# Two attention heads' start-up reordered: the next pair's cluster steps, one addition, one batch and the padding products

## The chip, the cores and the metric

One Trainium2 chip, one core in use. The metric is the device time of one execution in microseconds (us). The kernel before takes 450.0 us (median of three runs: 449.5, 450.0 and 450.33).

## The reference, cut to what matters

Sixteen heads (2 batches of 8) of attention over 768 positions with 64 dimensions, each masked so that a query sees only keys of its own cluster. Clusters come from an argmax against 16 normed centroids. The output is sent through a top-1 mixture of 8 experts.

```python
q_assign = np.argmax(np.einsum('bhsd,hcd->bhsc', q_n, c_n), axis=-1)
k_assign = np.argmax(np.einsum('bhsd,hcd->bhsc', k_n, c_n), axis=-1)
mask = q_assign[:, :, :, None] == k_assign[:, :, None, :]
scores = scale * np.matmul(q, k.transpose(0, 1, 3, 2))
scores = np.where(mask, scores, -1000000000.0)
scores = scores - np.max(scores, axis=-1, keepdims=True)
attn = np.exp(scores)
attn = attn / (np.sum(attn, axis=-1, keepdims=True) + 1e-09)
return np.matmul(attn, v)          # then logits = x @ w_gate, one expert per row: relu(x w1) w2
```

## The kernel before, in words

The heads go in pairs (head 0 and 1 are pair 0). Operands are stored transposed, in tiles that hold a high part, correction pieces, 16 mask rows for the cluster (so that the product itself adds a large negative number where clusters differ) and one row with the negated row maximum. The tiles are called `W`, `Y1`, `Qs` and `Y0`; a number behind the name tells the head's copy apart.

For each head there are 12 tiles of *maxima*: `max_tile` (line 344) makes a 128 x 384 product `m` on TensorE (L351), and VectorE reduces it to one column of `mx` (L358). `m` lives in two pools of PSUM, `psM` with two buffers and `psS` with three; a product into a buffer waits for the reduction of the tile that held it. When a head's maxima are complete, VectorE joins them (`max_half` L370 in two halves for head 0, `max_chain` L364 for the others, `mxx`), TensorE turns them into a row (`half_row` L381, `max_rows` L391), and ScalarE writes the row into `Qs` (L382), or a DMA does (L393, L394). Only then can `st_group` (line 406) finish a score tile: product L415 from `Y1` and `W`, product L416 from `Y0` and `Qs`, and the exponential L420 on ScalarE. In `high` (L1258) ScalarE copies a head's high part. `split` makes the correction pieces: a subtraction on GpSimd (L311) and DMAs on SyncE's queue (L321).

After the exponentials come the products with the values (`pv_batch`, L441, two batches of three key tiles; one key tile takes four passes in two concurrent pairs) and the row sums: `p_add` (L426) adds two of the three key tiles of a batch on VectorE, and `sum_strips` (L467) sums over partitions on TensorE.

The clusters of a pair: `cl_scores` (L183; one step per tile of 128 positions, two products of 96 columns), then `cl_assign`, a generator of four stages on VectorE: maximum L246; comparison L249 and multiplication L251; maximum L254; comparison L259 that writes the one-hot tile `ohb`. `cl_back` turns `ohb` (L286), ScalarE scales it into `qkm` (L294), and four DMAs bring its rows into the `W` and `Y1` tiles of both heads (L300).

Nothing may be reordered by a scheduler here: `keep` pins an engine's program order, so the order of the code is the order on each engine. `prologue` (line 1171) holds the start, `opening` (line 1260) all of head 0's score groups, with the maxima of heads 0 and 1 and the first three of head 2 between them. From head 1 on, a regular loop makes one score group, one or two maxima (`ahead`) and what `hooks` lists. `first_max` (line 1253) makes a maximum of head 0, `ahead` the next one of the following heads.

`keep_warm` (line 1132) makes 128 x 128 products in fp32 that nobody reads; each shows as two passes. `WARM1`, `WARM2` and `WARM3` are their counts at `first_max`, `half_row` and the first score group.

Of the kernel before, what the change touches and what calls it, by code (L numbers as in the profile page):

```python
# [7 lines left out]
F32 = mybir.dt.float32  # L8
# [4 lines left out]
ALU = mybir.AluOpType  # L13
# [3 lines left out]
P = 128  # L17
# [6 lines left out]
def kernel(  # L24
# [13 lines left out]
    nc = tc.nc  # L38
    B, NP, _, S = qT.shape
# [3 lines left out]
    NT = S // P  # L43
# [8 lines left out]
    OOB = 1 << 16  # L52
    NA = 4
    WARM1 = 1
    WARM2 = 2
    WARM3 = 3
    G_B0, G_B1, G_TURN, G_OUT = 8, 2, 5, 11
    TWICE = {(1, 1), (1, 2), (3, 2), (3, 3)}
# [71 lines left out]
    def keep(ins):  # L130
        if held[0] and ins.ins.engine in HELD:
            tc.keep_in_program_order(ins)
# [44 lines left out]
    def cl_scores(pi, w=1, t0=0, t1=NT):  # L177
        hp = pi % NP
        if t0 == 0:
            cl[pi] = psT.tile([P, 512], F32, tag="t", name="ctp")  # L180
        for t in range(t0, t1):
            for n, nm in enumerate("qk"):
                keep(nc.tensor.matmul(  # L183
                    out=cl[pi][:, t * 64 + n * 32:t * 64 + (n + w) * 32],
                    lhsT=pair[pi][nm][:, t * P:(t + 1) * P],
                    rhs=cbs[:, hp:hp + w, :],
                    start=True,
                    stop=True,
                ))
# [98 lines left out]
    def cl_back(pi):  # L288
        cl_back_turn(pi)
        cl_back_send(pi)  # L290
# [76 lines left out]
    def max_half(h, j):  # L367
        mx = mxt[h, j] = work.tile([P, TH], F32, tag="mxp", name="mxp")
        ts = slice(j * TH, (j + 1) * TH)
        keep(nc.vector.tensor_tensor(out=mx, in0=mxt[h][:, 0, ts], in1=mxt[h][:, 1, ts], op=ALU.max))  # L370
        if j == 1:
            mxt.pop(h)

    def half_row(h, j, warm=0):
        mx = mxt.pop((h, j))
        br = MROW[h % 2]
        tp = psO.tile([P, 512], F32, tag="o", name="mtd")
        if warm:
            keep_warm(warm, tp)
        for t in range(TH):  # L380
            keep(nc.tensor.transpose(tp[0:1, t * P:(t + 1) * P], mx[:, t:t + 1], ident))  # L381
        keep(nc.scalar.activation(  # L382
            out=pick(Qs_t, h)[br:br + 1, j * HALF:(j + 1) * HALF], in_=tp[0:1, 0:HALF], func=AF.Copy, scale=-1.0
        ))
# [12 lines left out]
    pt = {}  # L397
# [23 lines left out]
            out=pt[h, u][:, slot[0], slot[1]], in_=s[:, 0:HALF], func=AF.Exp, scale=1.0 / float(D) ** 0.5  # L421
        ))

    def p_add(h, u):
        a = acc[h, u] = work.tile([P, 2, HALF], F32, tag="acc", name="acc", bufs=3)
        keep(nc.vector.tensor_tensor(out=a, in0=pt[h, u][:, 0], in1=pt[h, u][:, 1], op=ALU.add))  # L426

    def p_add_rest(h, u):
        a, b = (x.rearrange("p j n -> p (j n)") for x in (acc[h, u], pt[h, u][:, 2]))
# [702 lines left out]
    def keep_warm(n, d):  # L1132

        for _ in range(n):
            keep(nc.tensor.matmul(out=d[:, 0:P], lhsT=onef, rhs=onef, start=True, stop=True))
# [35 lines left out]
    def prologue():  # L1171
# [5 lines left out]
        load_pair(0, ("k",))  # L1177
        load_pair(1)
        nc.scalar.activation(out=nbig2, in_=onef[:, 0:1], func=AF.Sqrt)
        keep_warm(5, psM.tile([P, 512], F32, tag="m", name="warm"))  # L1180
        for lst in (W_t, Y1_t, Qs_t, Y0_t):
            zero_rows(lst, 0)
        one_row(0, 0)
# [38 lines left out]
        cl_back0("q", tq)  # L1222
        mask0("q", tq, 0, slice(0, S), nc.scalar)
        high(2)
        cl_scores(1, 3, 2, 5)
        cl_back0("k", tk)
        cl_scores(1, 3, 5, NT)
        keep_warm(2, psM.tile([P, 512], F32, tag="m", name="warm"))
        for j in range(2):
            mask0("k", tk, 0, slice(j * HALF, (j + 1) * HALF), nc.scalar)  # L1230
# [9 lines left out]
        split(2, 2)  # L1240
        for k in range(NT):
            first_max(k)
        max_half(0, 0)
        a1 = gens["c"] = cl_assign(1, nc.vector)
        for j in range(2):
# [1 line left out]
        split(2, 4)  # L1247
        for k in range(NT, NT + 2):
            first_max(k, psM, "m")
        next(a1)  # L1250
        half_row(0, 0, WARM2)

    def first_max(k, *pool):
        max_tile(0, k // 2, k % 2, *(pool or ((psS, "s") if k % 5 < 3 else (psM, "m"))), warm=WARM1 if k in (3, 4, 5) else 0)

    def high(h):
        a = MAIN[h % 2]
# [2 lines left out]
    def opening():  # L1260
        a1 = gens.pop("c")
        load_pair(2)
        for g in range(2 * NT):
            if g == 6:
                half_row(0, 1)
            if g == 9:
                cl_back(1)
            if g == 10:
                pv_batch(0, 0)
            st_group(0, g)  # L1270
            if g < 4:
                first_max(8 + g, psM, "m")
            else:
                ahead()
            if g == 0:
                next(a1)
            if g == 3:
                max_half(0, 1)
            if g in (4, 6):
                next(a1, None)  # L1280
            if g == 8:
                high(3)
        split(3, 0, high=False)
        ahead(2)
        ahead(2, None, psS, "s")
        p_add(0, 0)
        p_add(0, 1)
        pv_batch(0, 1, range(1))
        max_rows(1)
        split(3, 1)  # L1290
        pv_batch(0, 1, range(1, TH))
        split(3, 2)
        split(3, 3)
        ahead(2)
        ahead(1, None, psS, "s")
        sum_strips(0)
        sum_evict(0)
        pv_evict(0)

# [4 lines left out]
    def ahead(n=1, at=None, *pool):  # L1304
        for _ in range(n):
            if maxima:
                m, k = maxima.pop(0)
                max_tile(m, k // 2, k % 2, *pool)
                if k == 2 * NT - 1:
                    max_chain(m)  # L1310
                    if at is not None:
                        rows_at[at + 2] = m
# [104 lines left out]
```

## Time and profile before

| What | Value |
|---|---|
| median of three runs | 450.0 us |
| the profiled execution | 449.91 us |
| its span | 448.1 us |
| TensorE busy | 431.6 us, 96% of the span |
| VectorE busy | 323.1 us, 72% |
| ScalarE busy | 273.8 us, 61% |
| GpSimd busy | 157.0 us, 35% |
| mean granted TensorE clock | 0.994 |

The span runs from the first to the last instruction; 1.8 us of the execution's time lie around it. PE is TensorE, DVE VectorE, ACT ScalarE, POOL GpSimd and SP SyncE. Matmuls are pipelined: a row shows a product from its start to its modelled end, so rows overlap, and what one product costs is read from start to start.

### The profile page before, as it was taken

How to read it: one execution, taken by the hardware profiler on the slowest of the kernel's cores; microseconds unless marked ns; L12 is line 12 of the kernel's file. 1: busy time of each engine (PE TensorE's matmuls, PEld its weight loads, DVE VectorE, ACT ScalarE, POOL GpSimd, SP SyncE). 2: the span in 40 equal slices, each digit the busy share in tenths (PEclk: the TensorE clock that was granted, in tenths of full speed). 3: DMA queues.
4: the chain of work that ended last, by engine and by line, in shares of the span. 5: the costliest groups of instructions: out<-in, count | busy, mean ns of one | idle time of the engine just before them, and what ended most of it. 6: DMA issues, size and time to landing. Idle time of an engine off the chain costs nothing. (4 is left out here: it accounts for less than half of the span.)

```text
span 448.1 us, 8089 instructions
## 1 busy us (share of the span) xinstructions
PE 431.6 (96%) x2776; PEld 343.2 (77%) x2776; DVE 323.1 (72%) x680; ACT 273.8 (61%) x550; POOL 157.0 (35%) x213
## 2 busy tenths in 40 slices
PE   8899999999999999999999998999999999999993
PEld 8755676676766767667665776999999999999972
DVE  4777968878788788888856644778777778786421
ACT  5655665756656557576665334668686868686330
POOL 7844665675655753573220500001010101011010
PEclk9999999999999999999999999899999999999999
DMA  6454476382763945347222367468787887975010
GB/s 194 126 150 151 105 236 215 86 292 81 213 217 104 308 145 156 81 126 225 68 98 88 144 221 233 139 219 259 250 262 251 247 260 229 281 242 187 27 40 19
DMA packets 31224, 78.14 MB, mean 174 GB/s; under 512 B 4678, under 2 KB 5024, under 8 KB 31172
## 3 DMA queue, kind: packets, MB, share of 16 engines
q1 hardware_dynamic: 26196, 61.18, 46.3%
q0 software_dynamic: 4832, 16.15, 9.7%
q8 instruction: 29, 0.48, 0.4%
q14 instruction: 23, 0.19, 0.2%
q10 hardware_dynamic: 144, 0.16, 0.1%
HBM read 50.46 MB, written 16.76 MB: 150 GB/s over the span
## 5 line engine op out<-in xcount | busy, mean ns | idle before, releaser
L358 DVE TENSOR_REDUCE mx<-m 128x1 f32<-128x384 f32 x192 | 102.5, 552 | 36.1 <-PE m L351 35.6
L420 ACT ACTIVATE pf<-s 128x384 f32<-128x384 f32 x192 | 89.5, 494 | 44.6 <-PE s L416 38.1
L142 DVE TENSOR_TENSOR ws<-wraw,ws 128x1024 fp32r<-128x1024 f32 x64 | 78.3, 1223 | 26.6 <-ACT ws L136 26.1
L697 POOL DMA_INDIRECT out_dram<-y,row x17 | 17.9, 1052 | 170.1 <-DMA row<-xd 79.7
L415 PE MATMUL s<-W,Y 112*128 112x384 f32 (+1 forms) x192 | 73.2, 381 | 0.0
L986 PE MATMUL g<-xc,ws 128*128 128x416 f32 x224 | 71.5, 379 | 1.5 <-DVE yT L995 0.6
L986 PE MATMUL g<-hc,ws 128*128 128x416 f32 x224 | 69.5, 371 | 0.0
L351 PE MATMUL m<-Y,W 112*128 112x384 f32 (+1 forms) x192 | 66.4, 353 | 2.0 <-DVE mx L358 1.4
L136 ACT ACTIVATE ws<-wraw 128x1024 fp32r<-128x1024 f32 x64 | 67.1, 1049 | 0.3 <-issue 0.2
L416 PE MATMUL s<-Qs,Y 97*128 97x384 f32 (+1 forms) x192 | 64.9, 338 | 0.4 <-ACT Qs L382 0.4
L441 PE MATMUL o<-pf,v 128*64 128x384 f32 x360 | 64.9, 495 | 0.0
L987 PE MATMUL g<-xc,ws 128*128 128x208 f32 x224 | 58.8, 262 | 1.8 <-issue 1.8
L987 PE MATMUL g<-hc,ws 128*128 128x208 f32 x224 | 57.9, 259 | 0.0
L415 PEld LDWEIGHTS s<-W,Y 112*128 112x128 f32 (+1 forms) x192 | 36.3, 189 | 16.7 <-issue 14.3
L994 ACT ACTIVATE pt<-g 128x208 f32<-128x208 f32 x84 | 27.4, 339 | 34.9 <-PE g L987 34.7
L432 POOL TENSOR_TENSOR acc<-acc,pf 128x256 f32<-128x256 f32 x39 | 29.6, 785 | 53.9 <-DVE acc L426 38.5
L986 PEld LDWEIGHTS g<-xc,ws 128*128 128x128 f32 x224 | 42.9, 192 | 3.6 <-issue 2.4
L987 PEld LDWEIGHTS g<-xc,ws 128*128 128x128 f32 x224 | 43.6, 195 | 2.0 <-issue 2.0
L441 PEld LDWEIGHTS o<-pf,v 128*64 128x64 f32 x360 | 23.4, 136 | 28.1 <-issue 23.5
L987 PEld LDWEIGHTS g<-hc,ws 128*128 128x128 f32 x224 | 42.8, 191 | 0.0
L986 PEld LDWEIGHTS g<-hc,ws 128*128 128x128 f32 x224 | 42.1, 188 | 0.4
L351 PEld LDWEIGHTS m<-Y,W 112*128 112x128 f32 (+1 forms) x192 | 35.9, 188 | 8.4 <-DVE mx L358 4.8
(210 smaller groups left out, 698.2 us busy)
## 6 DMA issues: line engine op xcount, KB each, us to landing
wraw<-in_w_dram SPq DMA_DIRECT2D x64, 512.0 KB, 4.3
xd<-z POOLq DMA_DIRECT2D x7, 780.0 KB, 6.0
row<-xd SPq DMA_DIRECT2D x18, 260.0 KB, 3.2
qv<-in_qT_dram SPq DMA_DIRECT2D x8, 384.0 KB
kv<-in_kT_dram SPq DMA_DIRECT2D x8, 384.0 KB, 3.6
Y<-Y SPq DMA_DIRECT2D x32, 96.0 KB, 2.2
Qs<-W SPq DMA_DIRECT2D x16, 192.0 KB, 6.8
v<-in_v_dram SPq DMA_DIRECT2D x8, 384.0 KB, 5.0
```

Of the source, the lines that this page charges most:

```text
L136: keep(nc.scalar.activation(out=w[:, 0], in_=raw[c], func=AF.Copy))
L142: keep(nc.vector.tensor_tensor(out=w[:, 1], in0=t, in1=w[:, 0].bitcast(F32), op=ALU.subtract))
L351: keep(nc.tensor.matmul(out=m[:, 0:HALF], lhsT=W[0:KA[h % 2], t * P:(t + 1) * P], rhs=Y1[0:KA[h % 2], j * HALF:(j + 1) * HALF], start=True ...
L358: keep(nc.vector.tensor_reduce(out=mxt[h][:, j, t:t + 1], in_=m[:, 0:HALF], axis=AX.X, op=ALU.max))
L415: keep(nc.tensor.matmul(out=s[:, 0:HALF], lhsT=Y1[0:ka, ks], rhs=W[0:ka, qs], start=True, stop=False))
L416: keep(nc.tensor.matmul(out=s[:, 0:HALF], lhsT=Y0[0:kb, ks], rhs=Qs[0:kb, qs], start=False, stop=True))
L420: keep(nc.scalar.activation(out=pt[h, u][:, slot[0], slot[1]], in_=s[:, 0:HALF], func=AF.Exp, scale=1.0 / float(D) ** 0.5))
L432: keep((nc.vector if u else nc.gpsimd).tensor_tensor(out=a[:, c:c + w], in0=a[:, c:c + w], in1=b[:, c:c + w], op=ALU.add))
L441: keep(nc.tensor.matmul(out=ot[h][j * D:(j + 1) * D, 0:HALF], lhsT=vt[h // 2][:, h % 2, kt, :], rhs=pf[:, n, j], start=(kt == 0), stop=(kt ...
L986: nc.tensor.matmul(out=o, lhsT=w[0], rhs=x.rearrange("p o n -> p (o n)"), start=start, stop=False)
L987: nc.tensor.matmul(out=o[:, 0:RW], lhsT=w[1], rhs=x[:, 0], start=False, stop=stop)
L994: nc.scalar.activation(out=t, in_=o[:, RW:2 * RW], func=AF.Copy)
```

## The change

In `prologue` two of the six steps of `cl_scores` for pair 1 move: the step with index 4, which stood ahead of the turned keys (`cl_back0("k", tk)`), and the one with index 5 behind them. They now stand behind the third and the fifth maximum of head 0. The first stage of `cl_assign` for pair 1 moves from behind the eighth maximum to behind the twelfth; the stages behind it move too. The ninth maximum of head 0 moves ahead of the first `half_row` and into the pool `psS`. In `opening` `ahead` is left out at two of the groups, and one tile is put into the first batch of value products. That batch now stands before `cl_back(1)`; the second batch is cut two to one around `max_rows(1)`, where it was one to two. `sum_strips(0)` stands ahead of the three maxima of head 2. `p_add(0, 0)` goes to GpSimd in three pieces of 256 columns. `high(3)` and the first subtraction of `split(3, 0)` follow group 8.

Of the padding, one fp32 product is added at the start, `WARM1` is used at one maximum instead of three, and in `half_row` twelve products of 32 columns in bf16 take the place of two fp32 ones; the second `half_row` gets twelve too.

```diff
-    WARM2 = 2
+    WARM2 = 12
...
-        if warm:
-            keep_warm(warm, tp)
+        for _ in range(warm):
+            keep(nc.tensor.matmul(out=tp[:, 0:32], lhsT=oneb, rhs=oneb[:, 0:32], start=True, stop=True))
...
-    def p_add(h, u):
+    def p_add(h, u, eng=nc.vector):
         a = acc[h, u] = work.tile([P, 2, HALF], F32, tag="acc", name="acc", bufs=3)
-        keep(nc.vector.tensor_tensor(out=a, in0=pt[h, u][:, 0], in1=pt[h, u][:, 1], op=ALU.add))
+        o, x, y = (t.rearrange("p j n -> p (j n)") for t in (a, pt[h, u][:, 0], pt[h, u][:, 1]))
+        w = S if eng is nc.vector else 256
+        for c in range(0, S, w):
+            keep(eng.tensor_tensor(out=o[:, c:c + w], in0=x[:, c:c + w], in1=y[:, c:c + w], op=ALU.add))
...
-        keep_warm(5, psM.tile([P, 512], F32, tag="m", name="warm"))
+        keep_warm(6, psM.tile([P, 512], F32, tag="m", name="warm"))
...
-        cl_scores(1, 3, 2, 5)
+        cl_scores(1, 3, 2, 4)
         cl_back0("k", tk)
-        cl_scores(1, 3, 5, NT)
...
         for k in range(NT):
             first_max(k)
+            if k in (2, 4):
+                cl_scores(1, 3, 3 + k // 2, 4 + k // 2)
...
-        next(a1)
+        first_max(NT + 2, psS, "s")
         half_row(0, 0, WARM2)
...
-warm=WARM1 if k in (3, 4, 5) else 0)
+warm=WARM1 if k == 4 else 0)
...
         for g in range(2 * NT):
             if g == 6:
-                half_row(0, 1)
-            if g == 9:
-                cl_back(1)
-            if g == 10:
-                pv_batch(0, 0)
-            st_group(0, g)
-            if g < 4:
-                first_max(8 + g, psM, "m")
-            else:
-                ahead()
-            if g == 0:
-                next(a1)
-            if g == 3:
-                max_half(0, 1)
-            if g in (4, 6):
-                next(a1, None)
-            if g == 8:
-                high(3)
-        split(3, 0, high=False)
+                half_row(0, 1, WARM2)
+            if g == 10:
+                pv_batch(0, 0, range(2))
+                ahead()
+                pv_batch(0, 0, range(2, TH))
+                cl_back(1)
+            st_group(0, g)
+            if g < 3:
+                first_max(9 + g, psM, "m")
+            elif g not in (5, 8):
+                ahead()
+            if g == 2:
+                max_half(0, 1)
+                next(a1)
+            if g in (4, 7):
+                next(a1)
+            if g == 8:
+                next(a1, None)
+                high(3)
+                split(3, 0, high=False)
+            if g == 9:
+                p_add(0, 0, nc.gpsimd)
         ahead(2)
         ahead(2, None, psS, "s")
-        p_add(0, 0)
         p_add(0, 1)
-        pv_batch(0, 1, range(1))
+        pv_batch(0, 1, range(2))
         max_rows(1)
         split(3, 1)
-        pv_batch(0, 1, range(1, TH))
+        pv_batch(0, 1, range(2, TH))
         split(3, 2)
         split(3, 3)
+        sum_strips(0)
         ahead(2)
         ahead(1, None, psS, "s")
-        sum_strips(0)
```

VectorE, from the join of head 0's first six maxima (`mxp`) to the one-hot tile of pair 1 (`ohb`), before:

```order
L370 TENSOR_TENSOR mxp<-mx 128x3
L358 TENSOR_REDUCE mx<-m 128x1 x2
L246 TENSOR_REDUCE cmx<-ctp 128x24
L358 TENSOR_REDUCE mx<-m 128x1
L249 TENSOR_TENSOR ceq<-ctp,cmx 128x384
L251 TENSOR_TENSOR ceq<-ceq,c16b 128x384
L358 TENSOR_REDUCE mx<-m 128x1 x3
L370 TENSOR_TENSOR mxp<-mx 128x3
```

And now:

```order
L370 TENSOR_TENSOR mxp<-mx 128x3
L358 TENSOR_REDUCE mx<-m 128x1 x6
L370 TENSOR_TENSOR mxp<-mx 128x3
L246 TENSOR_REDUCE cmx<-ctp 128x24
L358 TENSOR_REDUCE mx<-m 128x1 x2
L249 TENSOR_TENSOR ceq<-ctp,cmx 128x384
L251 TENSOR_TENSOR ceq<-ceq,c16b 128x384
```

The three cluster operations that stood between the reductions of head 0 stand behind all of them.

TensorE, from the last five maxima of head 1 to the first score group of head 1, before (`o` is the value product, `mtp` the turned maxima of head 1, `rsp` the row sums):

```order
L351 MATMUL m<-Y_103,W_99 128x384 x5
L441 MATMUL o<-pf,v 64x384 x2
L391 MATMUL mtp<-cs,mxx 6x128
L441 MATMUL o<-pf,v 64x384 x4
L351 MATMUL m<-Y_102,W_98 128x384 x3
L467 MATMUL rsp<-acc,onef 32x384 x2
L467 MATMUL rsp<-pf,onef 32x384 x2
L467 MATMUL rsp<-acc,onef 32x384 x2
L467 MATMUL rsp<-pf,onef 32x384 x2
L415 MATMUL s<-W_99,Y_103 128x384
```

And now:

```order
L351 MATMUL m<-Y_103,W_99 128x384 x5
L444 MATMUL o<-pf,v 64x384 x4
L391 MATMUL mtp<-cs,mxx 6x128
L444 MATMUL o<-pf,v 64x384 x2
L470 MATMUL rsp<-acc,onef 32x384 x2
L470 MATMUL rsp<-pf,onef 32x384 x2
L470 MATMUL rsp<-acc,onef 32x384 x2
L470 MATMUL rsp<-pf,onef 32x384 x2
L351 MATMUL m<-Y_102,W_98 128x384 x3
L415 MATMUL s<-W_99,Y_103 128x384
```

Two value products moved ahead of the turned maxima, and the row sums moved ahead of head 2's first maxima.

SyncE's queue, from the first load for head 3 to the row of maxima of head 1, before:

```order
L321 DMA Qs_108<-W_100 64x768
L300 DMA W_98<-qkm 16x768
L300 DMA Y_102<-qkm 16x768
L300 DMA W_100<-qkm 16x768
L300 DMA Y_104<-qkm 16x768
L321 DMA W_100<-ql 32x768
L394 DMA Qs_107<-mr 1x6x128
```

And now:

```order
L321 DMA Qs_108<-W_100 64x768
L321 DMA W_100<-ql 32x768
L321 DMA Qs_108<-ql 32x768
L300 DMA W_98<-qkm 16x768
L300 DMA Y_102<-qkm 16x768
L300 DMA W_100<-qkm 16x768
L300 DMA Y_104<-qkm 16x768
L394 DMA Qs_107<-mr 1x6x128
```

Two DMAs that wait for GpSimd's subtraction `ql` of head 3 now stand ahead of the four that bring the cluster rows.

## Rows read from the trace of the kernel before

**Rows 1.** Busy time by stretch, all engines, 50 to 100 us (busy and instructions)

```profile
50.00:100.00 50.00, 49.87 (x331) 33.77 (x330) 40.47 (x84) 30.65 (x64) 34.41 (x48) 1.00 0.59 183
```

**Rows 2.** Timeline of TensorE, 8 to 52 us: start, duration, instruction, [idle before <- what ended it]

```profile
14.21 0.64 PE L1135 MATMUL warm<-onef 128*128 128x128 f32 x4
14.60 0.90 PE L351 MATMUL m<-Y,W 112*128 112x384 f32 x3
...
18.26 0.49 PE L381 MATMUL mtd<-cs,mxp 128*1 128x128 f32 x3
...
21.06 0.34 PE L416 MATMUL s<-Qs,Y 97*128 97x384 f32 x1
22.39 0.44 PE L351 MATMUL m<-Y,W 112*128 112x384 f32 x1 [0.99 <-DVE mx L358]
22.67 0.34 PE L415 MATMUL s<-W,Y 112*128 112x384 f32 x1
22.84 0.34 PE L416 MATMUL s<-Qs,Y 97*128 97x384 f32 x1
...
26.42 0.39 PE L351 MATMUL m<-Y,W 128*128 128x384 f32 x1
26.84 0.51 PE L286 MATMUL ctb<-idb,ohb 128*128 128x128 bf16 x6
...
32.66 0.87 PE L441 MATMUL o<-pf,v 128*64 128x384 f32 x4
34.16 0.27 PE L391 MATMUL mtp<-cs,mxx 128*6 128x128 f32 x1 [0.64 <-DVE mxx L364]
...
37.96 0.44 PE L415 MATMUL s<-W,Y 128*128 128x384 f32 x1
```

**Rows 3.** Timeline of VectorE, same stretch

```profile
15.06 2.88 DVE L358 TENSOR_REDUCE mx<-m 128x1 f32<-128x384 f32 x6 [2.23 <-PE m L351]
17.98 0.16 DVE L370 TENSOR_TENSOR mxp<-mx 128x3 f32<-128x3 f32 x1
...
21.05 0.82 DVE L251 TENSOR_TENSOR ceq<-ceq,c16b 128x384 bf16<-128x384 bf16 x1
...
23.46 0.53 DVE L370 TENSOR_TENSOR mxp<-mx 128x3 f32<-128x3 f32 x1
...
34.02 1.82 DVE L426 TENSOR_TENSOR acc<-pf 128x768 f32<-128x768 f32 x2
```

**Rows 4.** Timeline of ScalarE, same stretch

```profile
13.79 1.03 ACT L279 ACTIVATE Y<-ctk,nbig 16x384 fp32r<-16x384 bf16 x2 [0.30 <-PE ctk L269]
```

**Rows 5.** Timeline of TensorE around 174 us: five small products in bf16

```profile
173.97 0.28 PE L640 MATMUL gps<-goh,oneb 128*128 128x80 bf16 x5
174.11 0.20 PE L641 MATMUL gps<-run,oneb 128*128 128x96 bf16 x1
```

**Rows 6.** Timeline of GpSimd, 8 to 52 us

```profile
23.20 2.10 POOL L311 TENSOR_TENSOR Y<-kv,Y 64x256 fp32r<-64x256 f32 x3
...
49.27 2.42 POOL L432 TENSOR_TENSOR acc<-acc,pf 128x256 f32<-128x256 f32 x3 [1.34 <-DVE cm L254]
```

**Rows 7.** Timeline of SyncE's queue, same stretch: issue of a DMA

```profile
29.02 0.52 SPq L300 DMA_DIRECT2D W<-qkm  x1
```

**Rows 8.** DMA issues, 5 to 60 us: issuer, count, KB each, median us to landing

```profile
W<-qkm SPq DMA_DIRECT2D x4, 48.0 KB, 2.0
```

**Rows 9.** Timeline of TensorE: three rows of the start, one around 278 us

```profile
1.05 2.50 PE L1135 MATMUL warm<-onef 128*128 128x128 f32 x10 [1.05 <-DVE nbig L1174]
3.83 0.58 PE L1144 MATMUL nps<-onef,csq 128*128 128x1 f32 x2 [0.28 <-DVE csq L1141]
...
8.57 1.90 PE L222 MATMUL ctp<-cbs,kv 128*128 128x128 f32 x12
...
278.20 0.37 PE L987 MATMUL g<-xc,ws 128*128 128x208 f32 x1 [1.78 <-issue]
```

**Rows 10.** Busy time by stretch, 279 to 283 us; the eighth figure is the granted clock

```profile
279.00:283.00 4.00, 4.00 (x19) 3.89 (x17) 2.17 (x4) 1.91 (x5) 0.00 (x0) 0.57 0.19 38
```

More of the change, by code (lines that the diff above doesn't have):

```diff
@@ L1249, in prologue @@
             first_max(k, psM, "m")
-        next(a1)
+        first_max(NT + 2, psS, "s")
         half_row(0, 0, WARM2)
     def first_max(k, *pool):
-        max_tile(0, k // 2, k % 2, *(pool or ((psS, "s") if k % 5 < 3 else (psM, "m"))), warm=WARM1 if k in (3, 4, 5) else 0)
+        max_tile(0, k // 2, k % 2, *(pool or ((psS, "s") if k % 5 < 3 else (psM, "m"))), warm=WARM1 if k == 4 else 0)
     def high(h):
```

## Prediction

> **What bounds the kernel now.** I read the busy time by stretch first. From 50 to 100 us TensorE is busy for 49.87 of 50 us [rows 1], while VectorE has 40.47 and ScalarE 30.65. So the regular part is TensorE's, and what a changed opening saves arrives at the end as an earlier start of that part. I take its start to be the first score product of head 1, at 37.96 [rows 2]; everything that the change moves lies ahead of it. Next I read TensorE's timeline up to there [rows 2], from start to start. Two products that follow each other without a wait stand 0.17 us apart (22.67, 22.84); right behind a wait the distance is 0.28 (22.39, 22.67). The reader should look for the places where more than that passes: 21.06 to 22.39, where a maximum waits for VectorE; 26.42 to 26.84, where the turn of the one-hot tile waits; and 32.66 to 34.16, where the turn of head 1's maxima waits. VectorE's timeline [rows 3] tells why. A reduction comes every 0.465 us ((2.88 - 0.55) / 5 for the six from 15.06, with 0.55 for the last), but between those of head 0 stand cluster operations, the longest of 0.82 at 21.05.
>
> **The change, part by part.** The sum is made against the profiled execution, 449.91 us, 0.09 below the median of 450.0. I lay the new order along the old durations.
>
> *A. Up to the turn of head 0's first six maxima*, which starts at 18.26 [rows 2]. One cluster step fewer stands ahead of the turned keys. ScalarE's key mask began at 13.79, behind an idle of 0.30 that the turned keys ended [rows 4]. It can start near 13.50, and the first maximum, which needs its first half (1.03 / 2), near 13.50 + 0.52 + 0.05 = 14.1. It started at 14.60, right behind four padding passes [rows 2], so VectorE is 0.5 early at first. But two cluster steps (four passes of 0.10 each; the four from 14.21 to 14.60 give the pass) now stand between the maxima, against two fp32 pads of two passes that go. The sixth product starts near 16.7, its reduction ends near 17.7, the join of 0.16 near 17.87. TensorE is then through with the ninth maximum and the twelve small products too (near 17.9), so the turn starts near 17.93. **Gain 0.33**, bounds 0 and 0.5.
>
> *B. From there to the second half row of head 0.* The last maxima of head 0 no longer find cluster operations between their reductions. The 1.33 from 21.06 to 22.39 becomes 0.17, and the distance behind it 0.17 instead of 0.28: 1.27. The ninth maximum is already made: 0.17. The second join ended at 23.46 + 0.53 = 23.99 [rows 3], where TensorE, with five more products of 0.175 behind 22.84, was ready at 23.72; that wait, 0.33 with 0.06 for the hand-over, goes. (The twelfth product now starts near 22.39 - 0.33 - 1.16 - 0.17 - 0.35, one score group fewer being ahead of it, so at 20.4; 0.44, a reduction of 0.55 and a join of at most 0.53 lead to 21.9, and TensorE arrives near 22.3.) The second twelve small products cost their time: 0.028 each, from five between 173.97 and 174.11 [rows 5], so 0.34. **Gain 1.27 + 0.17 + 0.33 - 0.34 = 1.43.** The trace has no such product in this place. One bound is 0; the other an fp32 pass of 0.10, with which all twenty-four cost 1.7 more. I take 0.028, since those five rows are bf16 against the same tile of ones.
>
> *C. The one-hot tile.* From 26.42 to 26.84 TensorE lost 0.42 - 0.18 = 0.24 [rows 2]. Now a score group (0.35) and the first value batch (2.3 with its inserted maximum) stand ahead of the turn, which comes near 26.84 - 1.76 - 0.24 + 0.35 + 2.3 = 27.5. VectorE's nine operations of about 0.5 behind the second join end near 26.5, so the wait goes. **Gain 0.24.** The price is that the cluster rows leave later. ScalarE's scaling of the turned tile, about 1.03 as for the same 768 columns at 13.79, ends near 29.1. On SyncE's queue two DMAs stand ahead that need GpSimd's subtraction for head 3. It starts behind `high(3)`, which stands ahead of the turn, so it ends at the latest 2.10 [rows 6] behind 27.5, at 29.6. Two issues and two for the first cluster rows, 0.52 or a little more each [rows 7], lead to 32.0 at the latest, and the row lands 2.0 behind its issue's start [rows 8], by 33.5. Head 2's first maximum needs them near 34.7. I charge nothing; 1.2 us are left.
>
> *D. Turned maxima of head 1, and the sums.* From 32.66 to 34.16 stands one key tile of value products, 0.70 with its hand-over; 0.80 was lost, 0.64 of it as the row's idle [rows 2]. A second key tile now fills 0.70. I leave 0.20 as a rest of the wait, since the join comes near 32.1. **Gain 0.60**, bounds 0 and 0.8. The first of the two additions on VectorE (1.82 for both at 34.02) [rows 3] goes to GpSimd: its three pieces take 2.42 [rows 6] and end by 32.0 at the latest. The row sums need them near 33.3, so the cover is 1.3 us.
>
> Here a rule speaks against the change. The join of three columns took 0.16 at 17.98 and 0.53 at 23.46 [rows 3], the latter while GpSimd's first piece ran from 23.20 to about 23.9 [rows 6]. So a two-input operation on VectorE can wait for a piece on GpSimd, for 0.8 at most (2.42 / 3). Until the join near 32.1 VectorE has reductions only, which read PSUM. I charge nothing, with 0.8 as the bound. The Trainium skill (SBUF — State Buffer, section "SBUF: two separate sides") calls the port that the two engines share an exclusive lock, held for a whole instruction while the other engine is blocked. The trace agrees (0.53 against 0.16); by that rule the sum stays the same unless a piece is still running at the join, and is then up to 0.8 smaller.
>
> *E. What comes back.* The first three maxima of head 2 stood ahead of the row sums, during which VectorE reduced them. Now they stand right ahead of head 1, whose next two groups make three more. The second maximum of group 1 waits for the reduction of group 0's, the fourth in line: 0.44 for the first product, 0.56 and three times 0.465 give 2.4 us, while TensorE gets there after nine products, about 1.9. Part of that wait was there before, since two maxima in a row always wait for each other. I charge 0.35 for it, and 0.10 because VectorE's remaining addition ends just when the sums want it. **Loss 0.45**, bounds 0 and 1.4 (three whole reductions).
>
> *At no cost:* the sixth padding product at the start. The ten passes from 1.05 end 0.28 ahead of the next product at 3.83, which waits for VectorE [rows 9]; two more, of some 0.21, fill the gap. If they are too long, at most 0.2 is lost.
>
> Sum: 0.33 + 1.43 + 0.24 + 0.60 - 0.45 = 2.15. So **449.91 - 2.15 = 447.8 us**. The uncertain terms together (A, the small products, D, E) leave a gain of 0.7 to 3.0: 446.9 to 449.2.
>
> **The rivals.** (1) *The clock rises earlier.* The first ten passes stand 0.21 to 0.25 apart (2.50 for ten) [rows 9], those from 14.21 0.10 [rows 2]: 1.2 GHz first, 2.4 later. The change falls inside the row of twelve from 8.57, whose 1.90 fits neither. The change closes the gap of 0.28 ahead of 3.83 [rows 9]. If the rise then comes by 6.3, ten passes on the way to the first cluster maximum save 0.11 each, 1.1 us on the path to the first mask: 446.7. Against it: the products behind that gap stay as they were. The Trainium skill (TensorE: Matmul & The Clock Gate, "Part 1: The HAM clock gate") says that the clock is low by default and that activity releases it. The trace agrees on both levels; no run so far shows whether one gap decides. Chance 0.18.
>
> (2) *The gain is eaten.* The small products cost 0.10 instead of 0.028 (1.7 lost), or VectorE's backlog takes the whole of E's bound and D gives nothing (1.55 lost). Then 449.5. For it: VectorE has 40.47 of 50 us to do in the regular part [rows 1], so a backlog drains slowly. Against it: rows 5. Chance 0.15.
>
> (3) *Slower: the clock falls in the opening.* Behind an idle of 1.78 at 278.20 [rows 9] the granted clock averages 0.57 from 279 to 283 [rows 10]: some 3.4 us at half, so up to 1.7 us of work lost. The change takes four fp32 padding products out of the stretch from 15 to 19 us and puts products of 32 columns there. If the clock fell twice in a row, 3.4 us would be lost against the 2.15: 451.2. One fall alone leaves 449.5, so the second decides. Against it: the longest idle left is about 0.5, and the old one of 0.99 at 22.39 brought no fall (the distances behind it are 0.28 and 0.17) [rows 2]. Chance 0.07.
>
> That the change doesn't do what it says is excluded by the order of the engines.
>
> **How the numbers follow.** A measurement of this kernel can tell about 0.2%, 0.9 us, from no change. The forecast has 0.60. The fall at 279 may also be missing in an execution, or come a second time, which moves one by up to 1.7. The range of 446.0 to 449.3 holds the forecast's bounds, the first rival and something of that, and leaves out the third and most of the second. Faster: 0.60 + 0.18 and a little of the second, 0.79. Within: the rest of the second, 0.14. Slower: 0.07.
>
> **What would show it.** In the profile of the changed kernel: no wait of 0.99 at a maximum of head 0; the turn of head 1's maxima near 32.3; the row sums right behind it; no wait for the cluster rows; head 1's first score product near 35.5; a wait for VectorE of about 0.5 in its second group; small products about 0.03 apart. I am wrong if that score product comes early and the end doesn't move with it, if the maxima of head 2 wait for a DMA, or if passes stand 0.21 apart in the opening behind 10 us.

## Result and the profile after

The changed kernel takes 445.1 us (median of four runs, 444.03 to 445.88) where the kernel before takes 450.2 us on the same chip (449.5 to 452.41). The ratio is 0.988, with a 95% interval of 0.984 to 0.992: faster, by 5.1 us. The forecast was 447.8 with a range of 446.0 to 449.3, so it had the sign and less than half of the size.

The profiled execution of the changed kernel took 444.03 us against 449.91, with a span of 442.0 us and a mean granted clock of 0.996. Its lines are three higher from `p_add` on (L426 is L429, L441 is L444, L467 is L470, L986 is L989, L1135 is L1138). I cut both executions at three products of TensorE:

| Stretch | before | after | gain |
|---|---|---|---|
| start to head 2's first score product | 50.65 | 47.80 | 2.85 |
| from there to the first product behind the jump into the expert stage (L986, now L989) | 224.74 | 225.46 | -0.72 |
| from there to the last product | 165.28 | 161.31 | 3.97 |
| from there to the end of the execution | 9.23 | 9.46 | -0.23 |

The sum is 5.87. The jump is a branch of TensorE (L1126, now L1129) over code that runs only where an expert got more rows. The regular part did what the prediction said of it (the same 49.87 of 50 us as in [rows 1]), but the largest gain lies far behind everything that the prediction summed.

Busy time by stretch in the changed kernel; the eighth figure is the granted clock:

```profile
50.00:100.00 50.00, 49.87 (x327) 33.75 (x328) 40.40 (x88) 31.30 (x67) 31.30 (x43) 1.00 0.64 200
274.00:278.00 4.00, 4.00 (x28) 3.98 (x28) 2.33 (x5) 2.57 (x7) 0.97 (x1) 1.00 0.70 249
```

The second row answers to [rows 10]: the clock of 0.57 is gone. TensorE's timeline around the jump, first of the kernel before, where the row at 278.20 of [rows 9] is the next one:

```profile
275.39 0.42 PE L986 MATMUL g<-xc,ws 128*128 128x416 f32 x1
...
276.05 0.37 PE L986 MATMUL g<-xc,ws 128*128 128x416 f32 x1
```

And of the changed kernel:

```profile
273.26 0.42 PE L989 MATMUL g<-xc,ws 128*128 128x416 f32 x1
...
273.92 0.37 PE L989 MATMUL g<-xc,ws 128*128 128x416 f32 x1
274.12 0.26 PE L990 MATMUL g<-xc,ws 128*128 128x208 f32 x1
```

Before, five products started behind the jump, and the sixth came 2.15 us after the fifth, put down to "issue": the profile shows nothing that it waited for. Now the sixth follows after 0.20. The opening, by TensorE's timeline of the changed kernel, which answers to [rows 2] and [rows 9]:

```profile
1.05 2.93 PE L1138 MATMUL warm<-onef 128*128 128x128 f32 x12 [1.05 <-DVE nbig L1177]
3.88 0.59 PE L1147 MATMUL nps<-onef,csq 128*128 128x1 f32 x2
...
13.38 1.08 PE L351 MATMUL m<-Y,W 112*128 112x384 f32 x3 [0.20 <-ACT Y L279]
...
16.80 0.47 PE L379 MATMUL mtd<-oneb 128*128 128x32 bf16 x12
17.11 0.49 PE L381 MATMUL mtd<-cs,mxp 128*1 128x128 f32 x3
...
19.34 0.34 PE L416 MATMUL s<-Qs,Y 97*128 97x384 f32 x1
19.52 0.38 PE L351 MATMUL m<-Y,W 112*128 112x384 f32 x1
...
26.34 0.87 PE L444 MATMUL o<-pf,v 128*64 128x384 f32 x4
27.13 0.51 PE L286 MATMUL ctb<-idb,ohb 128*128 128x128 bf16 x6
...
30.11 1.51 PE L444 MATMUL o<-pf,v 128*64 128x384 f32 x8
31.61 0.27 PE L391 MATMUL mtp<-cs,mxx 128*6 128x128 f32 x1
...
34.67 0.34 PE L415 MATMUL s<-W,Y 128*128 128x384 f32 x1
...
36.52 0.45 PE L351 MATMUL m<-Y,W 112*128 112x384 f32 x1 [0.41 <-DVE mx L358]
```

The reader should see the three waits of [rows 2] gone (at 19.52, 27.13 and 31.61 no idle is noted), the new one at 36.52, and the closed gap ahead of 3.88. VectorE's timeline there, which answers to [rows 3]:

```profile
16.78 0.20 DVE L370 TENSOR_TENSOR mxp<-mx 128x3 f32<-128x3 f32 x1
...
20.53 0.16 DVE L370 TENSOR_TENSOR mxp<-mx 128x3 f32<-128x3 f32 x1
...
31.48 0.95 DVE L429 TENSOR_TENSOR acc<-pf 128x768 f32<-128x768 f32 x1
34.52 3.58 DVE L358 TENSOR_REDUCE mx<-m 128x1 f32<-128x384 f32 x7 [2.09 <-PE m L351]
```

### The profile page after: what moved, and what is told of

Its sections match the earlier page's. It is cut to its first block, busy times and chain, and to the rows that moved or that the text cites. A ratio compares the mean times of both kernels' runs of the same rounds, so it can differ in the third digit from the quotient of the medians.

```text
span 442.0 us, 8127 instructions
## 1 busy us (share of the span) xinstructions
PE 428.0 (97%) x2794; PEld 340.0 (77%) x2794; DVE 320.6 (73%) x679; ACT 273.7 (62%) x550; POOL 159.8 (36%) x216
## 5 line engine op out<-in xcount | busy, mean ns | idle before, releaser
L989 PE MATMUL g<-xc,ws 128*128 128x416 f32 x224 | 70.0, 373 | 1.1 <-PEq L1129 0.3
L989 PE MATMUL g<-hc,ws 128*128 128x416 f32 x224 | 69.5, 371 | 0.0
L444 PE MATMUL o<-pf,v 128*64 128x384 f32 x360 | 65.1, 495 | 0.0
L444 PEld LDWEIGHTS o<-pf,v 128*64 128x64 f32 x360 | 23.3, 136 | 27.9 <-issue 23.0
L989 PEld LDWEIGHTS g<-xc,ws 128*128 128x128 f32 x224 | 42.1, 188 | 3.2 <-issue 2.8
L990 PEld LDWEIGHTS g<-xc,ws 128*128 128x128 f32 x224 | 42.8, 191 | 0.0
L989 PEld LDWEIGHTS g<-hc,ws 128*128 128x128 f32 x224 | 42.1, 188 | 0.4
```

Source lines behind the costliest of these rows:

```text
L444: keep(nc.tensor.matmul(out=ot[h][j * D:(j + 1) * D, 0:HALF], lhsT=vt[h // 2][:, h % 2, kt, :], rhs=pf[:, n, j], start=(kt == 0), stop=(kt ...
L989: nc.tensor.matmul(out=o, lhsT=w[0], rhs=x.rearrange("p o n -> p (o n)"), start=start, stop=False)
L990: nc.tensor.matmul(out=o[:, 0:RW], lhsT=w[1], rhs=x[:, 0], start=False, stop=stop)
```

## The experiments

**The question.** The theory that I formed from the two traces: the opening gives 2.2 us by the prediction's terms and some 0.7 more because the clock rises earlier; the rest comes from the *place of TensorE's code*. The profile counts DMA packets of the kind "instruction"; queue q8 has 29 pieces of 16,384 bytes, 0.48 MB in all. From 15.9 to 275.6 us of the kernel before thirteen of them come while TensorE starts 3,334 instructions, 256 to a piece, so they fit TensorE's program. The change adds 36 TensorE instructions net: 24 small products of two instructions (a weight load and a pass), less four fp32 products of four, plus one of four. All later code lies 36 instructions further along. The instruction queue, kernel before, 260.35 to 278.35 us (15 us ahead of the jump and 3 behind it):

```profile
q8 instruction: 1, 0.02, 0.4%
```

The same 18 us around the jump of the changed kernel, 258.2 to 276.2:

```profile
q8 instruction: 2, 0.03, 0.7%
```

Before, one piece comes, and only with the jump: it starts 0.23 us behind the first product there, and TensorE goes on 2.58 us behind its start. Now one comes 4.85 us ahead of the jump as well. The rival theories: the stall and the fall of the clock come and go by chance; or only how busy TensorE is ahead of the stage decides.

**1. The kernel before once more, before_again.** No edit.

> The kernel before, unchanged, for a second profile. Theory: the idle of 1.78 us at 276 to 278 us is TensorE waiting for its own code, whose place is fixed by the program; it is there again, and the granted clock falls behind it in this execution or not, as the moment has it. The clock in the start rises between 7.5 and 11 us. Rival: the idle is a chance of one execution; then it is gone here. Time 450 us by both, 448.5 if the clock doesn't fall.

Measured: 450.8 us, ratio 1.001 (0.999 to 1.003). Its profile shows 1.93 us from start to start behind the fifth product and the clock at half for 3.4 us. The stall is there again, at the same product: it isn't chance.

The fall of the clock behind it is, in part. The three profiles with the fall have a mean granted clock of 0.994 (b_pad6, below, is the third), the eleven without it 0.995 to 0.998. Of the 59 executions of the kernel before whose clock is on record beside these experiments, 19 have 0.994 or less, and on each of the three chips their median is 1.2 to 1.6 us over that of the others. So by the clocks the fall comes in about a third of the executions. The profile of before has it; a median holds it at most in part.

**2. Code moved, nothing else: b_code18.** The kernel before, with 18 small products (36 instructions) where TensorE waits for VectorE anyway, ahead of head 0's twelfth maximum.

```diff
+            if g == 3:
+                sp = psO.tile([P, 512], F32, tag="o", name="sp")
+                for _ in range(18):
+                    keep(nc.tensor.matmul(out=sp[:, 0:32], lhsT=oneb, rhs=oneb[:, 0:32], start=True, stop=True))
```

> The kernel before with 18 small products (36 instructions, as many as the change adds net) ahead of head 0's twelfth maximum, where TensorE waits for 1.2 us anyway; the opening stays as it is. Theory (place of the code): the idle of 1.78 us at 276 us goes and with it the fall of the clock: 449.9 - 1.8 - 1.5 = 446.6 us, with the first score product of head 1 still at 38.0. Rival (the opening alone explains all of the change, the idle at 276 is chance or due to what the DMAs do): 450 us.

Measured: 447.1 us against 449.8, ratio 0.994 (0.991 to 0.997). TensorE's timeline of this kernel, in the opening and at the jump:

```profile
21.68 0.62 PE L1274 MATMUL sp<-oneb 128*128 128x32 bf16 x18
22.37 0.44 PE L351 MATMUL m<-Y,W 112*128 112x384 f32 x1
...
277.47 0.37 PE L986 MATMUL g<-xc,ws 128*128 128x416 f32 x1
277.68 0.25 PE L987 MATMUL g<-xc,ws 128*128 128x208 f32 x1
```

The twelfth maximum starts at 22.37 as before (22.39), and head 2's first score product at 50.60 (50.65): the opening gained nothing. The sixth product behind the jump comes at once, the clock stays at 1.00, and two pieces stand in the 18 us around the jump. 2.7 us for code that computes nothing.

**3. The clock alone: b_pad6 and a_pad5.** The sixth padding product at the start, added to the kernel before and taken from the changed one.

```diff
-        keep_warm(5, psM.tile([P, 512], F32, tag="m", name="warm"))
+        keep_warm(6, psM.tile([P, 512], F32, tag="m", name="warm"))
```

> The kernel before with a sixth padding product at the start. Theory (the gap ahead of 3.83 us holds the clock down): the clock rises near 5 to 8 us instead of 9.4, the first maximum of head 0 comes near 13.7 instead of 14.6 and the time falls by 0.7 to 1.1 us, to 449.2. Rival (the moment of the rise is chance): rise near 9.4 again or anywhere, time 450.0 within 0.4.

> The changed kernel with five padding products at the start. Theory (gap): the clock rises near 9.4 us again or between 7.5 and 11, the first maximum comes near 14.1 instead of 13.4, the first score product of head 1 near 35.4 instead of 34.7, the time is 0.7 to 1.0 us over the changed kernel: 445.9. Rival: as the changed kernel, 445.1.

Measured: b_pad6 449.9 us, ratio 0.999 (0.998 to 1.001); a_pad5 445.0 us, ratio 0.989 (0.985 to 0.993). In b_pad6's profile the clock rises at 6.32 us instead of 9.40 and head 2's first score product comes at 49.54, 1.11 earlier, just as expected; in a_pad5 the rise is at 7.74 and that product 0.55 later than in the changed kernel. The second is not shown to be the clock's doing: the changed kernel's other profile, after2 (experiment 7), has the rise at 4.28 and that product at 48.40, behind a_pad5's 48.35 (see A below). Over all profiles the two groups don't overlap: five padding products, rise at 7.74 to 10.26 (five profiles); six, 4.14 to 6.32 (nine profiles). The medians show neither. In b_pad6's profile the gain is lost again on the way to the jump, which takes 1.33 longer than in before's, with a spacing of 1.67 us near 202 us that before lacks (see the last section). The stall at the jump is a little longer too, with four instructions more (TensorE's timeline):

```profile
275.61 0.42 PE L986 MATMUL g<-xc,ws 128*128 128x416 f32 x1
275.87 0.26 PE L987 MATMUL g<-xc,ws 128*128 128x208 f32 x1
275.97 0.37 PE L986 MATMUL g<-xc,ws 128*128 128x416 f32 x1
278.28 0.36 PE L987 MATMUL g<-xc,ws 128*128 128x208 f32 x1 [1.94 <-issue]
```

It is 2.31 from start to start instead of 2.15. What the earlier clock is worth in the median stays open.

**4. The opening alone: a_warm3.** The changed kernel with three small products per half row instead of twelve: 36 instructions fewer, so code lies as in the kernel before.

```diff
-    WARM2 = 12
+    WARM2 = 3
```

> The changed kernel with three small products instead of twelve at each of the two half rows: 36 instructions fewer on TensorE, so its code lies where it lay before the change. Theory (place of the code): the idle of about 2 us around 274 to 276 us and the fall of the clock behind it are back, while the opening keeps its gain or wins up to 0.25 more: 445.0 + 2.7 - 0.1 = 447.6 us, which is also the change of the opening alone, about 2.2 under before. Rival (padding is only padding): 444.8.

Measured: 446.2 us against 448.4, ratio 0.995 (0.993 to 0.997). TensorE's timeline:

```profile
272.93 0.43 PE L989 MATMUL g<-xc,ws 128*128 128x416 f32 x1
...
273.59 0.37 PE L989 MATMUL g<-xc,ws 128*128 128x416 f32 x1
275.37 0.25 PE L990 MATMUL g<-xc,ws 128*128 128x208 f32 x1 [1.41 <-issue]
```

The stall is back, behind the fifth product as in the kernel before, and what is left is 2.1 us, near the forecast's sum of 2.15; by its profile the opening gives 2.39 (head 2's first score product at 48.26). The clock did not fall behind this stall in the profiled execution.

**5. The same opening, code moved at the other end: a_w3shift.** a_warm3 with 18 small products at 256 us, ahead of the turn of a row whose load TensorE waits for.

```diff
-    WARM2 = 12
+    WARM2 = 3
...
-    def turn(src, hi, lo, pool, tag, parts=1):
+    def turn(src, hi, lo, pool, tag, parts=1, warm=0):
...
+        for _ in range(warm):
+            keep(nc.tensor.matmul(out=tp[:, 0:32], lhsT=oneb, rhs=oneb[:, 0:32], start=True, stop=True))
...
-                turn(rows[e, t][:, 0:DM], x[0], x[1], *pt_, parts=2 if sfx == "c" else 1)
+                turn(rows[e, t][:, 0:DM], x[0], x[1], *pt_, parts=2 if sfx == "c" else 1, warm=18 if sfx == "b" else 0)
```

> The changed kernel with three small products ahead of each half row in place of twelve, and 18 small products (36 instructions) put instead in front of the turn of the one row whose load TensorE waits 0.8 us for at about 257 us. 18 products of 0.026 us are 0.47 us and lie inside that wait. Theory (the place of the code decides): the stall of 1.77 us that the variant with three small products alone had at 273.6 us is gone and the time is 1.3 to 2.3 us under that variant's, so 2.1 to 4 us under the kernel before by the opening and the rest together: about 0.990 to 0.993 of the kernel before. Rival (the small products in the opening, or when the opening ends, decide whether TensorE stalls at 276 us): the stall of some 1.8 us stays and the time is 0.995 of the kernel before, as without the 18 products, or 0.2 us longer.

Measured: 443.8 us against 448.9, ratio 0.988 (0.987 to 0.990). TensorE's timeline:

```profile
255.97 0.61 PE L858 MATMUL rtp<-oneb 128*128 128x32 bf16 x18
256.84 0.66 PE L861 MATMUL rtp<-cs,row 128*128 128x128 f32 x4 [0.26 <-DMA row<-xd]
...
272.81 0.37 PE L991 MATMUL g<-xc,ws 128*128 128x416 f32 x1
273.01 0.25 PE L992 MATMUL g<-xc,ws 128*128 128x208 f32 x1
```

The products hide in the wait for the row (0.83 idle became 0.26), the stall is gone, two pieces come again, and the ratio falls by 0.67%, more than the expected 2.3 us at most. By the traces 2.2 of it lies behind the jump and 0.7 in an opening that came through earlier (A below says by what). The small products in the opening aren't needed for the stall to go; the place of the code is.

**6. The other direction: b_less12.** The kernel before without its three fp32 padding products between the maxima of head 0, 12 instructions fewer.

```diff
-    WARM1 = 1
+    WARM1 = 0
```

> The kernel before without the three fp32 padding products between head 0's maxima: 12 TensorE instructions fewer, so that later code lies 12 instructions nearer to the start. Theory (a piece of code that is asked for late at the jump; the passes there take about 0.15 us per 2 instructions): 12 more instructions can run before the code runs out, the idle time at about 277 us shrinks from about 2.1 us (start to start) to 1.1 to 1.5 us, and the time is 0.6 to 1.2 us shorter, or 2 to 3 us if the clock no longer falls behind it. Rival (any other place of the code is as good as that of the changed kernel): no stall at all. Second rival (the place of the code does not matter, only how busy TensorE is just ahead of the stage): 2.1 us of idle time and the fall as before.

Measured: 448.0 us against 448.9, ratio 0.998 (0.996 to 0.999). TensorE's timeline:

```profile
274.98 0.42 PE L986 MATMUL g<-xc,ws 128*128 128x416 f32 x1
...
276.53 0.37 PE L986 MATMUL g<-xc,ws 128*128 128x416 f32 x1
277.56 0.37 PE L987 MATMUL g<-xc,ws 128*128 128x208 f32 x1 [0.66 <-issue]
```

Eleven products run before the stall, where five did before. Six more products of two instructions each are exactly the 12. With b_pad6's four more instructions it was three products, two fewer: exact again. So the code runs out at a fixed place of the program, and this place says more than the time does. The gap shrank from 2.15 to 1.03 (start to start), for the next product comes 2.4 to 2.8 us behind the first one in every profile with the stall. The pieces of code go with it without an exception: in the five profiles with the stall one starts 0.13 to 0.31 us behind the first product, none comes in the 20 us ahead of it, and TensorE goes on 2.28 to 2.58 us behind its start; in the nine others one starts 4.0 to 4.9 us ahead of the jump.

What lies behind the jump can now be added up. From the first product there to the last one:

| Kernel | instructions against before | time behind the jump | first gap, second gap (some 20 us later) | clock at half |
|---|---|---|---|---|
| before | 0 | 165.28 | 2.15, 0.81 | 3.4 us |
| before_again | 0 | 165.09 | 1.93, 0.84 | 3.4 us |
| b_pad6 | +4 | 165.54 | 2.31, 0.92 | 3.4 us |
| a_warm3 | 0 | 163.52 | 1.77, 1.04 | no |
| b_less12 | -12 | 163.31 | 1.03, 1.25 | no |
| b_code18, a_w3shift | +36 | 161.30, 161.32 | none | no |
| after, after2, a_pad5, a_clback, a_sumback, a_dve, a_both | +36 (a_pad5 +32) | 161.30 to 161.32 | none | no |

Without the stall all nine profiles agree to 0.02 us. With it, the gaps (less 0.20 each, the usual distance) explain a_warm3 and b_less12 to within 0.2, and in the first three rows 1.4 us remain, the price of the clock's fall: 3.97 - 1.95 - 0.61 = 1.41 for before. Without it the stall costs before 2.56, which is near the 2.7 of b_code18's median.

The "no" in the last column is that of one execution. By the mean granted clock (0.994 or less) the fall comes in 6 of 10 executions of b_pad6, with the longest gap, 19 of 59 of the kernel before, 1 of 18 of a_warm3 and b_less12 together; and 3 of 45 without the stall are that low. So the longer gaps go with more frequent falls, and no gap here decides one.

**7. Single parts of the opening: a_clback, a_sumback, a_dve, a_both.** a_clback puts the first two stages of `cl_assign` back between head 0's reductions. a_sumback puts the row sums back behind head 2's three maxima. a_dve has both additions on VectorE. a_both is a_sumback and a_dve together.

```diff
+        next(a1)
         first_max(NT + 2, psS, "s")
+        next(a1)
         half_row(0, 0, WARM2)
...
             if g == 2:
                 max_half(0, 1)
-                next(a1)
             if g in (4, 7):
-                next(a1)
-            if g == 8:
                 next(a1, None)
+            if g == 8:
                 high(3)
                 split(3, 0, high=False)
```

```diff
-        sum_strips(0)
         ahead(2)
         ahead(1, None, psS, "s")
+        sum_strips(0)
```

```diff
-            if g == 9:
-                p_add(0, 0, nc.gpsimd)
...
+        p_add(0, 0)
         p_add(0, 1)
```

> The changed kernel with the first two cluster stages of pair 1 between the reductions of head 0 again, as they stood before (behind the eighth and the ninth maximum); TensorE's order and code stay the same. Theory (main term of B): the twelfth maximum waits for VectorE by 1.0 to 1.3 us again and all behind it comes later: 446.2 us. Rival (VectorE has the same work in either order and the wait comes elsewhere anyway): 445.0 within 0.3.

> The changed kernel with the row sums of head 0 behind the three maxima of head 2 again. Theory (term E, a backlog on VectorE): the wait of 0.41 us at the second maximum of head 1's group 1 goes, since VectorE reduces the three during the sums, and the sums wait for nothing because GpSimd's addition is long done: head 1's first score product as in the changed kernel (34.7 if the clock rises early), head 2's 0.4 earlier than there against it; 444.6 us. Rival (nothing to gain, the order of the two only shifts the wait): 445.0.

> The changed kernel with both additions of head 0 on VectorE. Theory: the two take 1.8 us behind the join of head 1's maxima, so the row sums start 0.8 later than now and wait for VectorE; 445.8 us. Rival (GpSimd's addition holds VectorE up by as much as it saves): 445.0 or less.

> The changed kernel with two parts undone that lay on head 1's beginning: head 0's first addition is on VectorE again (no instruction of GpSimd for it), and the column sums of head 0 stand behind the three maxima of head 2 as in the kernel before. Theory: the wait of 0.41 us at the second maximum of head 1's group 1 is gone as in the variant with the sums alone, and the addition on VectorE lies in its idle time there, so 0.3 to 0.8 us under the changed kernel of this job. Rival (with the sums late, VectorE's 0.87 us addition meets the next maxima): as the changed kernel, within 0.2 us.

> The changed kernel once more, beside the variants of this job. Theory (2.2 us from the first 50 us of the kernel, 0.7 of it by the clock that rises earlier, and about 2.7 us from TensorE's code that now lies otherwise at the jump into the expert stage): 4.4 to 5.6 us under the kernel before, head 2's first score at 47.8 us, no idle time of TensorE over 0.8 us and no fall of the clock between 270 and 285 us. Rival (the stall at 276 us and the fall behind it come and go by chance from one execution to the next): one or both are there in this profile or the times of the executions spread over 2 us.

Measured: a_clback 444.3 us (0.990, 0.989 to 0.992), a_sumback 444.05 (0.989, 0.988 to 0.991), a_dve 443.4 (0.989, 0.987 to 0.990); on another chip a_both 443.4 (0.988, 0.986 to 0.990) and the changed kernel itself, after2, 444.0 (0.989, 0.986 to 0.991). TensorE's timeline of a_clback:

```profile
19.27 0.34 PE L416 MATMUL s<-Qs,Y 97*128 97x384 f32 x1
20.58 0.44 PE L351 MATMUL m<-Y,W 112*128 112x384 f32 x1 [0.97 <-DVE mx L358]
```

The wait of [rows 2] is back, 1.31 from start to start, and head 2's first score product is 1.10 later than in the changed kernel, 1.19 later counted from the first turn. TensorE's timeline of a_sumback, at head 1's group 1:

```profile
35.48 0.90 PE L351 MATMUL m<-Y,W 112*128 112x384 f32 x2
36.22 0.34 PE L415 MATMUL s<-W,Y 128*128 128x384 f32 x1
```

Of the wait of 0.41 us 0.11 is left, as much as in the kernel before (0.12), too little to be noted in the row; from the first turn to head 2's first score product it takes 30.34 us, 0.35 less. VectorE's timeline of a_dve:

```profile
31.40 1.82 DVE L429 TENSOR_TENSOR acc<-pf 128x768 f32<-128x768 f32 x2
34.53 3.56 DVE L358 TENSOR_REDUCE mx<-m 128x1 f32<-128x384 f32 x7 [1.31 <-PE m L351]
```

My expectation of a loss fails: with both additions VectorE still has 1.31 of the idle time that was 2.09, and head 1's first score product stays at 34.68 (34.67). So the addition on GpSimd bought nothing that these profiles show. None of these four can be told from the changed kernel by time: a_both against after2 is 0.6 us with intervals that overlap almost wholly. No version here is shown to beat the changed kernel.

## Why the prediction was wrong, point by point

**What failed: the step that bounds the sum.** The prediction says that "everything that the change moves lies ahead" of head 1's first score product. Everything that the change computes does; but its 36 instructions move all code behind them, and that decided a stall at 276 us and with it whether the clock could fall behind it. [Rows 9] showed the stall, marked "issue", and [rows 10] the fall; the prediction used them only to price a rival and to widen its range. Size of the missing term: 3.97 us in the profiled pair (2.56 for the two gaps, 1.41 for the fall), 2.7 by b_code18's median, 2.2 between a_warm3's and a_w3shift's profiles. That the fall may miss in an execution, as the prediction says, is borne out: by the clocks it misses in about two of three.

Shown: that the place of the code decides the stall, in both directions and from two places of insertion, and that a piece of code comes with the jump in every profile that has the stall and ahead of it in every one that hasn't. That TensorE waits for this piece is read from the times alone; no row names what it waits for. Not shown: why the clock falls in one execution and not in another of the same kernel.

The Trainium skill (Runtime: NRT & Kernel Launch, section "Instruction fetch mechanics") says that an engine's program is refilled in blocks of 16 KiB, 256 instructions, mostly unseen, and that a taken branch whose target is in neither of the two pages held stalls the engine. The trace agrees on the size of a piece (16,384 bytes, 256 instructions) and that TensorE can stall behind a jump, here with a first gap of 1.03 to 2.31 us; but the target's first 3 to 11 products ran, and only the code behind them was late.

**A (up to the first turn, 0.33): too small, with one duration wrong.** The turn starts at 17.11, 1.15 earlier. The first maximum was forecast near 14.1 and came at 13.38; the 0.72 between them goes with rival 1, whose chance was 0.18: the clock rose at 4.79, with the gap closed. The rival's price of 1.1 us stood against b_pad6's 1.11 in the opening. That this explains the profile is luck. The prediction took 0.16 for the join of head 0's first six maxima, which the turn needs, and priced a wait for GpSimd only at head 1's join. GpSimd in the changed kernel, where the join at 16.78 took 0.20:

```profile
16.23 2.12 POOL L311 TENSOR_TENSOR Y<-kv,Y 64x256 fp32r<-64x256 f32 x3
```

GpSimd, VectorE and TensorE in after2, the same kernel once more:

```profile
16.23 2.10 POOL L311 TENSOR_TENSOR Y<-kv,Y 64x256 fp32r<-64x256 f32 x3
16.91 0.76 DVE L370 TENSOR_TENSOR mxp<-mx 128x3 f32<-128x3 f32 x1
...
17.72 0.49 PE L381 MATMUL mtd<-cs,mxp 128*1 128x128 f32 x3 [0.33 <-DVE mxp L370]
```

The three pieces take 0.70 each in both. The join at 16.78 ended with the first of them, the one at 16.91 with the second. In all fourteen profiles this join ends 0.01 to 0.06 us behind the end of a piece, and in eight of the nine with the change's opening it takes 0.61 to 0.76. So a join that comes 0.13 later moves the turn by 0.6: in after2 A gives 0.54, in the profiled execution 1.15. after2's opening gains 2.25 (head 2's first score product at 48.40 against 50.65), where the profiled execution gained 2.85; a_w3shift's turn stands one piece ahead of a_warm3's (17.02, 17.73).

**B, C, D (1.43, 0.24, 0.60): right in their sum.** From the first turn to head 1's first score product it took 19.70 and takes 17.56 now: 2.14, against 2.17 forecast (the three less E's 0.10). In before_again it took 19.09, with the turn 0.65 later, so the gain is 1.5 to 2.1, with the forecast at its upper end. B's main cause is shown by a_clback (1.19 from the first turn come back, of 1.27). The twelve small products take 0.31 (16.80 to 17.11), 0.026 each where [rows 5] gave 0.028. The one-hot tile and the turned maxima wait for nothing (27.13, 31.61; the forecast of 32.3 less 0.72 is 31.58).

**E (-0.45): right.** The wait stands at the named maximum. Head 1's start to head 2's takes 13.13 instead of 12.69, and a_sumback gives 0.35 of it back. Head 1's join, at which the prediction charged a wait for GpSimd at nothing, took 0.17 in all fourteen profiles: right there, but not at head 0's (A).

**The rivals.** The second (gain eaten) is out: the small products are cheap and the backlog cost what E said. The third (the clock falls in the opening) didn't happen in any profile. A fourth was missing: that code which shifts can take a stall away, or bring one. And the lower end of the gain, 0.7, is not what the stated bounds add up to: with A and D at nothing, the small products at 0.10 and E at 1.4 they make a loss of 1.4.

## What to carry to other kernels

An idle time of an engine that the profile puts down to "issue", a few products behind a jump, may be its own program arriving late. Count the instructions that an edit adds or removes ahead of it, look at the instruction queue around the jump, and test with padding that hides in a wait: 18 products here were worth 2.7 us. Compare two versions of one stage only after asking whether they moved the code behind it. And take a second profile of the same kernel before an explanation rests on a few tenths: here 0.6 us of an opening hung on which piece of GpSimd's work a join met.

## What the runs showed of the hardware that I had not expected

The stall's place follows the instruction count exactly: 3, 5 and 11 products behind the jump for 4 more, 0 more and 12 fewer instructions. A second gap some 20 us later (0.81 to 1.25 from start to start) is there and gone with the first.

A gap of 0.07 to 0.37 us behind the padding at the start (five profiles) goes with a rise of the clock to 2.4 GHz at 7.74 us or later; without it (nine profiles) the rise comes by 6.32.

A join of three columns on VectorE, 0.16 us at its shortest, takes up to 0.76 beside GpSimd's subtractions of 0.70 us each; the first such join ends within 0.06 us of the end of one of them in each of the fourteen profiles.

In five of the fourteen profiles, of kernels before and after alike, TensorE's spacing opens near 202 us to 0.65 to 1.68 us; four of the five (before_again, b_code18, b_pad6, a_pad5) come from one chip, and none of the eight from two other chips has it. In the changed kernel it is this row of TensorE's timeline, 0.97 behind the start of the one ahead:

```profile
203.18 0.44 PE L351 MATMUL m<-Y,W 112*128 112x384 f32 x1 [0.64 <-DVE mx L358]
```

It eats 0.8 of the gain in the second stretch of the first table. What causes it wasn't tried.
